# Attention stage: keys transposed in fp32 with the low part taken from the bank, and state products in fp32

## The chip, the cores and the metric

The kernel runs on one core of one Trainium2 chip. The metric is the device time of one execution in microseconds (us); less is better. The three runs shown of the kernel before took 1138.49, 1142.32 and 1143.38 us, median 1142.32.

## What is computed

The program computes a retention layer (attention without a softmax, with a decay for each head), and two mixture-of-experts layers behind it. The change touches the first layer alone:

```python
# q, k, v: [8 batches, 8 heads, 576 positions, 64], float32
scores = (1 / sqrt(64)) * q @ k.transpose(0, 1, 3, 2)
gamma  = 1.0 - 2.0 ** (-5.0 - arange(8))            # one decay for each head
Dmat   = where(i >= j, gamma ** (i - j), 0.0)       # i, j: positions
attn   = (scores * Dmat) @ v
x      = attn, as [4608 tokens, 512]
x      = moe(x)     # 8 experts, each token to its best one
out    = moe2(x)    # 8 experts, each with a fixed share of the tokens
```

## The kernel before

**Tiles.** The 4608 tokens are cut into 36 tiles of 128, all 8 heads of a tile at once. A batch has four whole tiles and a tail of 64 positions; the tails of two batches share a tile, so 32 tiles are whole and 4 are tails. Inside a tile the scores are computed outright (`scores`, `outputs`). What earlier tiles of the batch add comes from a 64x64 state for each head, the decayed sum of the products of keys and values, which `kv` carries from tile to tile (tails need no new state).

**Precision.** TensorE multiplies float16. Each fp32 operand is kept as a high part and a low part (the rounding error of the high part), and a product is the sum of three: high by high, high by low, low by high.

**Stages.** The list `stages` (L304) names what is done in a step of the loop at L305, and with which lead: loads 6 tiles ahead (`load`), decayed values on GpSimd 4 ahead (`pre`, `vf`), splits of k and v 3 ahead (`kvsplit`), transposes of q and k 2 ahead (`trans`), scores 1 ahead, then state (`kv`), `outputs` and the scaled rows `xr` (`rows`), the transposed rows 1 behind (`xtrans`) and the logits of the router 2 behind. A scheduler with a model of the engines sets the final order on each queue, so the order of the code isn't that of the engines.

**The key's way before.** ScalarE writes the high part `kh` of the loaded k (L146), VectorE the low part `kl` (L147), both with the positions on partitions. TensorE turns both in float16, eight transposes of 128x128 into one PSUM bank (L176), and ScalarE copies the bank to SBUF as `kT` in one instruction of 128x1024 (L177). `kv` multiplies `kh`, `kl` with `vh`, `vl`: 24 float16 products a tile, each with 64 columns of weights and 64 moving columns, two heads side by side on the two halves of the partitions (L230).

**The query's way**, for comparison: four fp32 transposes (`across`, L156), ScalarE takes the high part from the bank (L162), TensorE subtracts it in the bank (L163), ScalarE takes the rest (L164). The rows `xr` go the same way.

**PSUM.** `tp` has three banks that transposes of q, k and rows and the logits share; `pS` (two banks, one buffer) holds the scores, `pO` (two banks) the output, `pk` one bank the state's products. `pS` is used thus: 24 score products (L189), VectorE writes the masked high part `sh` (L192), TensorE subtracts it in the bank (L194), VectorE writes the low part `sl` (L196); only then do the next tile's scores start.

Of the kernel before, what the change touches and what calls it, by code (L numbers as in the profile page):

```python
# [9 lines left out]
F32 = mybir.dt.float32  # L10
F16 = mybir.dt.float16
I32 = mybir.dt.int32
AF = mybir.ActivationFunctionType
OP = mybir.AluOpType
# [27 lines left out]
def consts_np():  # L42
    import numpy as np
    p=np.arange(128)
    g=1.0-2.0**(-5.0-np.arange(8))
    cols=[]
    cols.append((g[None,:]**(127-p)[:,None])*256.0)
    cols.append((g[None,:]**(63-p%64)[:,None])*256.0)
    cols.append((g[None,:]**(p-127.0)[:,None])*2.0**-21)
    cols.append((g[None,:]**((p%64)-63.0)[:,None])*2.0**-21)  # L50
    hd=(np.arange(4)[None,:]*2+(p[:,None]//64))
    cols.append(g[hd]**128*2.0**-6); cols.append(g[hd]**64*2.0**-6)
    tok=np.zeros((128,36))
    for t in range(36):
        pr,k=divmod(t,9)
        if k<8:
            c,bi=divmod(k,2); tok[:,t]=(2*pr+bi)*576+c*128+p
        else: tok[:,t]=(2*pr+p//64)*576+512+p%64
    cols.append(tok)
    cols.append(np.eye(128))  # L60
    j=p[:,None]; i=p[None,:]
    cols.append((i>=j)*2.0**-6)
    cols.append(((i>=j)&((i//64)==(j//64)))*2.0**-6)
    cols.append((j<i)*1.0)
    cols.append((1.0*p)[:,None])
    cols.append((p[:,None]//16==np.arange(8)[None,:])*1.0)
    cols.append((p[:,None]%16==np.arange(16)[None,:])*1.0)
    return np.ascontiguousarray(np.concatenate(cols,1).astype(np.float32))
# [32 lines left out]
def attention(k, q, kk_, v, wg1, X, after):  # L101
    tc, nc = k.tc, k.nc
    from contextlib import ExitStack
    ctx = ExitStack()
    ld = ctx.enter_context(tc.tile_pool(name="ld", bufs=4))
    wk = ctx.enter_context(tc.tile_pool(name="wk", bufs=3))
    xp = ctx.enter_context(tc.tile_pool(name="xrp", bufs=4))
    ps = ctx.enter_context(tc.tile_pool(name="aps", bufs=1, space=bass.MemoryType.PSUM))
# [18 lines left out]

    def load(d):
        for src, name in ((kk_, "k"), (q, "q"), (v, "v")):
            t = ld.tile([128, 8, 64], F32, name=name, bufs=5 if name == "q" else 3)  # L130
            if d.tail:
                for bi in range(2):
                    nc.sync.dma_start(t[bi * 64:(bi + 1) * 64], src[2 * d.pr + bi, :, 512:576, :].rearrange("h p d -> p h d"))
            else:
                nc.sync.dma_start(t, src[d.b, :, d.c * 128:(d.c + 1) * 128, :].rearrange("h p d -> p h d"))
            setattr(d, "i" + name, t)

    def pre(d):

        d.vf = wk.tile([128, 8, 64], F32, name="vf", bufs=3)  # L140
        nc.gpsimd.tensor_tensor(d.vf, d.iv, k.c('gkt' if d.tail else 'gk')[:, :, None].to_broadcast([128, 8, 64]), op=OP.mult)

    def kvsplit(d):
        d.kh = wk.tile([128, 8, 64], F16, name="kh", bufs=5)
        d.kl = wk.tile([128, 8, 64], F16, name="kl", bufs=4)
        nc.scalar.activation(d.kh, d.ik, AF.Copy, scale=256.0)  # L146
        nc.vector.scalar_tensor_tensor(d.kl, d.ik, 256.0, d.kh, op0=OP.mult, op1=OP.subtract)  # L147
        d.vh = wk.tile([128, 8, 64], F16, name="vh", bufs=4)
        d.vl = wk.tile([128, 8, 64], F16, name="vl", bufs=4)
        nc.scalar.activation(d.vh, d.vf, AF.Copy)  # L150
        nc.gpsimd.tensor_tensor(d.vl, d.vf, d.vh, op=OP.subtract)  # L151

    def across(pt, x):

        for c in range(4):
            nc.tensor.matmul(pt[:, c, :], x[:, c * 128:(c + 1) * 128], idf, is_transpose=True, start=c == 0, stop=False,  # L156
                             skip_group_check=True)

    def split(h, l, pt):

        f = lambda x: x.rearrange("p c i -> p (c i)")
        nc.scalar.activation(h, pt, AF.Copy, scale=256.0)  # L162
        nc.tensor.matmul(f(pt), k.less8, f(h), start=False, stop=True, skip_group_check=True)  # L163
        nc.scalar.activation(l, pt, AF.Copy, scale=256.0)  # L164

    def trans(d):
        d.qh, d.ql = (wk.tile([128, 4, 128], F16, name=x, bufs=4) for x in ("qTh", "qTl"))
        pt = ps.tile([128, 4, 128], F32, name="tp", bufs=3)
        across(pt, d.iq.rearrange("p a d -> p (a d)"))
        split(d.qh, d.ql, pt)  # L170
        kT = wk.tile([128, 2, 4, 128], F16, name="kT", bufs=2)
        d.kTh, d.kTl = kT[:, 0], kT[:, 1]
        pt = ps.tile([128, 2, 4, 128], F16, name="tp", bufs=3)
        for n, x in enumerate((d.kh, d.kl)):
            for hp in range(4):
                nc.tensor.transpose(pt[:, n, hp, :], x[:, 2 * hp:2 * hp + 2, :].rearrange("p a d -> p (a d)"), k.idh)  # L176
        nc.scalar.activation(kT, pt, AF.Copy)  # L177

    def scores(d):

# [17 lines left out]
    state = {}  # L198
# [22 lines left out]
    def kv(d):  # L221
        d.state = dict(state)
        if d.tail:
            return
        pk = ps.tile([128, 4, 64], F32, name="pk")
        for hp in range(4):
            for n, (x, y) in enumerate(((d.kh, d.vh), (d.kh, d.vl), (d.kl, d.vh))):
                for z in range(2):
                    h = 2 * hp + z
                    nc.tensor.matmul(pk[64 * z:64 * z + 64, hp, :], x[:, h, :], y[:, h, :], start=n == 0, stop=n == 2)  # L230
        f = k.c('gst' if d.c == 3 else 'gs')[:, :, None].to_broadcast([128, 4, 64])
        n32 = wk.tile([128, 4, 64], F32, name=f"st{d.bi}", bufs=2)
        nh = wk.tile([128, 4, 64], F16, name=f"sth{d.bi}", bufs=2)
        nl = wk.tile([128, 4, 64], F16, name=f"stl{d.bi}", bufs=2)
        if d.c:
            s1 = wk.tile([128, 4, 64], F32, name="s1", bufs=3)
            nc.vector.scalar_tensor_tensor(s1, state[d.bi][0], 64.0, pk, op0=OP.mult, op1=OP.add)
            nc.gpsimd.tensor_tensor(n32, s1, f, op=OP.mult)
        else:
            nc.vector.tensor_tensor(n32, pk, f, op=OP.mult)  # L240
        nc.scalar.activation(nh, n32, AF.Copy)
        nc.gpsimd.tensor_tensor(nl, n32, nh, op=OP.subtract)
        state[d.bi] = (n32, nh, nl)
# [55 lines left out]
    def store(n):  # L299
        for _ in range(min(n, len(pend))):  # L300
            t, xr = pend.pop(0)
            nc.sync.dma_start(Xv[:, t, :], xr)

    stages = [(load, -6), (pre, -4), (trans, -2), (xtrans, 1), (kvsplit, -3), (scores, -1), (kv, 0), (outputs, 0), (rows, 0), (logits, 2)]  # L304
    for s in range(-7, NT + 5):  # L305
        store(2 if s < NT + 2 else 36)
        for f, off in stages:
# [1285 lines left out]
def program(tc, q, kk, v, wg1, w11, w12, wg2, w21, w22, consts, out, dbg=None):  # L1593
    nc = tc.nc
    ctx = ExitStack()
    k = K()
    k.pin = False
    setup(k, tc, nc, ctx, consts)
    moe_setup(k, ctx)
    X = tc.dram_tile([128 * NT, W], F32, name="Xs")  # L1600
    X1 = tc.dram_tile([128 * NS, W], F32, name="X1s")
    LG = tc.dram_tile([128 * NS, 8], F32, name="LGsd")
    g1 = split_gate(k, wg1, "wg1")
    k.wgl = split_gate(k, wg2, "wg2")
    select_setup(k)
    k.w = {0: K()}
    attention(k, q, kk, v, g1, X, early(k, X, w11[0]))
    open_ffn(k)
    rest = moe1(k, X, X1, w11, w12)
    k.pin = False  # L1610
    overflow(k, X, X1, LG, w11, w12)
    k.wn, k.xn, k.yn = 8, 9, 0
    k.pin = True
    moe2(k, X1, w21, w22, out, rest)
    k.pin = False
    anew(k, X1, w21, w22, out)
    if dbg:
        dbg(k, X, X1, LG)
    k.fctx.close()
    ctx.close()  # L1620
# [25 lines left out]
```

## Time and profile before

| | us |
|---|---|
| median of three runs | 1142.32 |
| the profiled execution, its own time | 1138.98 |
| its span, first to last instruction | 1137.1 |
| masked scores `sh`, start of the first and of the last of 36 | 12.5, 223.6 |
| PE busy | 1063.3 |
| DVE busy | 679.8 |
| ACT busy | 512.0 |
| POOL busy | 351.7 |

PE is TensorE's products, PEld its weight loads, DVE is VectorE, ACT ScalarE, POOL GpSimd, SP the queue that issues nearly all transfers. A matmul's end is modelled and products are pipelined, so PE reads as busy for longer than its array works. The mean granted clock of TensorE is 0.983. The first 230 us are the attention stage; the mixture-of-experts layers take the rest.

### The profile page before, as it was taken

To read this page: it belongs to the slowest core of one execution; us is meant where nothing else is said; L and a number is where in the kernel's file an instruction comes from. 1 tells how busy PE (TensorE), PEld (TensorE's weight loads), DVE (VectorE), ACT (ScalarE), POOL (GpSimd) and SP (SyncE) were. 2 spreads that over 40 slices of the span, in tenths; PEclk is the share of its full clock that TensorE was granted. 3 is DMA by queue.
4 is the path that set the end of the run, shared out by engine and by line. 5 is a ranking of instruction groups with operands and counts; after the bars stand their busy time and mean duration, and the time that the engine had idled before them with its cause. 6 is when DMAs were issued, how large, how long until landed. Compare 5 with 4: busy or idle time off the path is not lost. (4 is left out here: it accounts for less than half of the span.)

```text
span 1137.1 us, 26608 instructions
## 1 busy us (share of the span) xinstructions
PE 1063.3 (94%) x10679; PEld 680.3 (60%) x10679; DVE 679.8 (60%) x1662; ACT 512.0 (45%) x887; POOL 351.7 (31%) x589
## 2 busy tenths in 40 slices
PE   6899999888999999999989999898999999899996
PEld 4677777645556565656457644556475656567573
DVE  5788788766466655656544366748575666634140
ACT  6788787646354445545433123323232322224231
POOL 6767566322203020202031023234233051441101
PEclk9999999989999999999989999899999999999998
DMA  9979885439767676767967024357375473784211
GB/s 233 241 184 238 186 194 132 104 113 235 184 161 198 145 195 166 195 159 206 241 144 126 19 91 143 116 140 162 117 214 143 137 184 109 185 205 138 90 62 44
DMA packets 307523, 178.37 MB, mean 157 GB/s; under 512 B 241408, under 2 KB 274176, under 8 KB 307392
## 3 DMA queue, kind: packets, MB, share of 16 engines
q1 hardware_dynamic: 296928, 144.24, 52.0%
q0 software_dynamic: 10464, 32.34, 9.1%
q8 instruction: 87, 1.43, 0.5%
q14 instruction: 44, 0.36, 0.1%
HBM read 116.82 MB, written 31.28 MB: 130 GB/s over the span
## 5 line engine op out<-in xcount | busy, mean ns | idle before, releaser
L505 PE MATMUL ph<-xT,w1h 128*128 128x320 f16 (+4 forms) x2048 | 369.9, 297 | 14.4 <-DVE sc L318 7.1
L505 PEld LDWEIGHTS <-w1h 128*128 128x128 f16 x2048 | 198.6, 99 | 89.5 <-issue 26.0
L505 PE MATMUL ph<-xT,w1l 128*128 128x320 f16 (+4 forms) x1024 | 231.7, 297 | 0.0
L531 PE MATMUL py<-w2h,hh 128*128 128x512 f16 x536 | 203.2, 379 | 4.3 <-DVE x1r L587 2.2
L531 PE MATMUL py<-w2l,hh 128*128 128x512 f16 x536 | 203.2, 379 | 0.0
L531 PE MATMUL py<-w2h,hl 128*128 128x512 f16 x536 | 203.2, 379 | 0.0
L531 PEld LDWEIGHTS <-hh 128*128 128x128 f16 x1072 | 103.1, 98 | 121.6 <-issue 6.3
L510 ACT ACTIVATE hh<-ph 128x576 f16<-128x576 f32 (+4 forms) x136 | 83.3, 614 | 178.7 <-PE ph L505 174.1
L511 DVE SCALAR_TENSOR_TENSOR hl<-ph,hh 128x576 f16<-128x576 f32 (+4 forms) x136 | 97.8, 719 | 66.1 <-ACT hh L510 64.9
L505 PEld LDWEIGHTS <-w1l 128*128 128x128 f16 x1024 | 100.0, 99 | 33.0 <-issue 1.6
L393 DVE SCALAR_TENSOR_TENSOR w1l<-stage,w1h 128x1024 f16<-128x1024 f32 x62 | 75.9, 1228 | 60.5 <-ACT w1h L390 59.4
L531 PEld LDWEIGHTS <-hl 128*128 128x128 f16 x536 | 52.4, 98 | 60.3
L393 DVE SCALAR_TENSOR_TENSOR w2l<-stage,w2h 128x1024 f16<-128x1024 f32 x64 | 78.4, 1225 | 10.2 <-ACT w2h L390 8.9
L436 ACT ACTIVATE x1r<-py 128x512 bf16<-128x512 f32 x40 | 23.8, 596 | 109.0 <-PE py L531 65.5
L390 ACT ACTIVATE w2h<-stage 128x1024 f16<-128x1024 f32 x64 | 67.0, 1049 | 6.8 <-DMA stage<-in_moe_w_dram 6.7
L390 ACT ACTIVATE w1h<-stage 128x1024 f16<-128x1024 f32 x62 | 64.2, 1046 | 9.4 <-DMA stage<-in_moe_w_dram 9.4
L1452 POOL DMA_INDIRECT out_dram<-w2T,ti x20 | 21.8, 1089 | 128.3 <-ACT w2T L1451 107.6
L589 POOL COPY x1r<-sc 128x1 f32<-128x1 f32 x37 | 8.3, 227 | 163.2 <-DMA X1s<-x1r 102.2
L1452 POOL DMA_INDIRECT out_dram<-x1r,ti x20 | 21.4, 1072 | 120.6 <-ACT x1r L1451 101.8
L424 POOL DMA_INDIRECT xg<-X1s,ix x40 | 45.2, 1129 | 43.1 <-DVE zf L1378 23.4
L192 DVE TENSOR_TENSOR sh<-pS,ct 128x1024 f16<-128x1024 f32 x36 | 43.8, 1217 | 16.1 <-PE pS L189 16.1
L151 POOL TENSOR_TENSOR vl<-vf,vh 128x512 f16<-128x512 f32 x36 | 42.6, 1186 | 31.4 <-ACT vh L150 30.9
(376 smaller groups left out, 1900.7 us busy)
## 6 DMA issues: line engine op xcount, KB each, us to landing
stage<-in_moe_w_dram SPq DMA_DIRECT2D x128, 512.0 KB, 4.2
Xs<-xr SPq DMA_DIRECT2D x36, 257.0 KB, 4.5
X1s<-x1r SPq DMA_DIRECT2D x33, 257.0 KB, 3.7
k<-in_k_dram SPq DMA_DIRECT2D x32, 256.0 KB, 4.0
q<-in_q_dram SPq DMA_DIRECT2D x32, 256.0 KB, 4.2
v<-in_v_dram SPq DMA_DIRECT2D x32, 256.0 KB, 4.2
q<-in_q_dram SPq DMA_DIRECT2D x8, 128.0 KB, 3.8
k<-in_k_dram SPq DMA_DIRECT2D x8, 128.0 KB, 4.9
```

The costliest lines, as they stand in the source:

```text
L151: nc.gpsimd.tensor_tensor(d.vl, d.vf, d.vh, op=OP.subtract)
L192: nc.vector.tensor_tensor(f(d.sh), f(pS), both, op=OP.mult)
L390: d = nc.scalar.activation(at(h, i), t, AF.Copy, scale=128.0)
L393: d = nc.vector.scalar_tensor_tensor(at(l, i), t, 128.0, at(h, i), op0=OP.mult, op1=OP.subtract)
L424: nc.gpsimd.indirect_dma_start(out=xg[:M], out_offset=None, in_=src, in_offset=bass.IndirectOffsetOnAxis(ap=gidx[:M], axis=0))
L436: d = nc.scalar.activation(q.bitcast(mybir.dt.bfloat16), x, AF.Square, accum_out=sc[:, 0:1])
L505: pe(k, nc.tensor.matmul(ph[:, z, :b], x[:, c, F], xT[:, y + c, a:a + b], start=i == 0, stop=i == 11))
L510: nc.scalar.activation(oh, src, AF.Relu)
L511: nc.vector.scalar_tensor_tensor(ol, src, 0.0, oh, op0=OP.max, op1=OP.subtract)
L531: pe(k, nc.tensor.matmul(py, x[:, f, S], y[:, f, :], start=i == 0, stop=i == 23))
L589: nc.gpsimd.tensor_copy(xr[:, 513:514], sc[:, 5:6])
L1452: nc.gpsimd.indirect_dma_start(out=out2 if tail else out, out_offset=bass.IndirectOffsetOnAxis(ap=ti, axis=0), in_=y, in_offset=None)
```

## The change

- ScalarE and VectorE no longer split the loaded k: `kh` and `kl` go, `kvsplit` becomes `vsplit`, for v alone.
- Four fp32 transposes turn the loaded k into a `tp` bank (L170 of the new file); ScalarE writes the high part `kTh` from the bank, 128x512, and VectorE writes the low part `kTl` from the bank and `kTh`, 128x512 (L172).
- `kv` multiplies the loaded k and the decayed v in fp32: 8 products a tile in place of 24. The scales of the state follow (k is no longer multiplied by 256).
- k and `vf` are now read by `kv` and so are held longer: 7 buffers for k in place of 3, 5 for `vf` in place of 3.

```diff
-    cols.append(g[hd]**128*2.0**-6); cols.append(g[hd]**64*2.0**-6)
+    cols.append(g[hd]**128*4.0); cols.append(g[hd]**64*4.0)
...
-            t = ld.tile([128, 8, 64], F32, name=name, bufs=5 if name == "q" else 3)
+            t = ld.tile([128, 8, 64], F32, name=name, bufs=dict(k=7, q=5, v=3)[name])
...
-        d.vf = wk.tile([128, 8, 64], F32, name="vf", bufs=3)
+        d.vf = wk.tile([128, 8, 64], F32, name="vf", bufs=5)
...
-    def kvsplit(d):
-        d.kh = wk.tile([128, 8, 64], F16, name="kh", bufs=5)
-        d.kl = wk.tile([128, 8, 64], F16, name="kl", bufs=4)
-        nc.scalar.activation(d.kh, d.ik, AF.Copy, scale=256.0)
-        nc.vector.scalar_tensor_tensor(d.kl, d.ik, 256.0, d.kh, op0=OP.mult, op1=OP.subtract)
+    def vsplit(d):
...
-        pt = ps.tile([128, 2, 4, 128], F16, name="tp", bufs=3)
-        for n, x in enumerate((d.kh, d.kl)):
-            for hp in range(4):
-                nc.tensor.transpose(pt[:, n, hp, :], x[:, 2 * hp:2 * hp + 2, :].rearrange("p a d -> p (a d)"), k.idh)
-        nc.scalar.activation(kT, pt, AF.Copy)
+        pt = ps.tile([128, 4, 128], F32, name="tp", bufs=3)
+        across(pt, d.ik.rearrange("p a d -> p (a d)"))
+        nc.scalar.activation(d.kTh, pt, AF.Copy, scale=256.0)
+        nc.vector.scalar_tensor_tensor(d.kTl, pt, 256.0, d.kTh, op0=OP.mult, op1=OP.subtract)
...
-            for n, (x, y) in enumerate(((d.kh, d.vh), (d.kh, d.vl), (d.kl, d.vh))):
-                for z in range(2):
-                    h = 2 * hp + z
-                    nc.tensor.matmul(pk[64 * z:64 * z + 64, hp, :], x[:, h, :], y[:, h, :], start=n == 0, stop=n == 2)
+            for z in range(2):
+                h = 2 * hp + z
+                nc.tensor.matmul(pk[64 * z:64 * z + 64, hp, :], d.ik[:, h, :], d.vf[:, h, :], start=True, stop=True)
...
-            nc.vector.scalar_tensor_tensor(s1, state[d.bi][0], 64.0, pk, op0=OP.mult, op1=OP.add)
+            nc.vector.scalar_tensor_tensor(s1, state[d.bi][0], 0.25, pk, op0=OP.mult, op1=OP.add)
...
-    stages = [(load, -6), (pre, -4), (trans, -2), (xtrans, 1), (kvsplit, -3), (scores, -1), (kv, 0), (outputs, 0), (rows, 0), (logits, 2)]
+    stages = [(load, -6), (pre, -4), (trans, -2), (xtrans, 1), (vsplit, -3), (scores, -1), (kv, 0), (outputs, 0), (rows, 0), (logits, 2)]
```

The scheduler orders the changed program anew. On VectorE, in the first third of the attention stage, before (numbers tell buffers apart; `pS_624` to `sh_622` to `sl_623` is one tile):

```order
L147 SCALAR_TENSOR_TENSOR kl_477<-k_205,kh_476 128x512
L192 TENSOR_TENSOR sh_622<-pS_624,ct_58 128x1024
L251 TENSOR_TENSOR xr_435<-pO_686,ct_58 128x2x4x64
L196 TENSOR_TENSOR sl_623<-pS_624,ct_58 128x1024
L147 SCALAR_TENSOR_TENSOR kl_615<-k_242,kh_614 128x512
L192 TENSOR_TENSOR sh_797<-pS_799,ct_58 128x1024
L251 TENSOR_TENSOR xr_435<-pO_861,ct_58 128x2x4x64
L147 SCALAR_TENSOR_TENSOR kl_790<-k_310,kh_789 128x512
L196 TENSOR_TENSOR sl_798<-pS_799,ct_58 128x1024
```

and of the change, in the same part of the stage (`kT` is written from the bank `tp`):

```order
L191 TENSOR_TENSOR sl_1010<-pS_1011,ct_58 128x1024
L172 SCALAR_TENSOR_TENSOR kT_1159<-tp_1160,kT_1159 128x512
L187 TENSOR_TENSOR sh_1181<-pS_1183,ct_58 128x1024
L245 TENSOR_TENSOR xr_953<-pO_1229,ct_58 128x2x4x64
L172 SCALAR_TENSOR_TENSOR kT_1313<-tp_1314,kT_1313 128x512
L191 TENSOR_TENSOR sl_1182<-pS_1183,ct_58 128x1024
L231 SCALAR_TENSOR_TENSOR s1_1378<-st1_1049,pk_1366 128x256
L187 TENSOR_TENSOR sh_1335<-pS_1337,ct_58 128x1024
L245 TENSOR_TENSOR xr_953<-pO_1383,ct_58 128x2x4x64
```

The low part of the key stands at the same places, once a tile between `sl` and the next `sh` or between `xr` and `sl`; it now waits for a bank and for ScalarE's `kTh`.

On TensorE, around the transposes of q and k, before, in the second half of the stage:

```order
L156 MATMUL tp<-ct,q 128x128 x4
L176 LDWEIGHTS kh
L176 MATMUL tp<-idh,kh 128x128
...
L176 LDWEIGHTS kl
L176 MATMUL tp<-idh,kl 128x128
...
L230 LDWEIGHTS kh
L230 MATMUL pk<-vh,kh 64x64
...
L194 LDWEIGHTS less_65
L194 MATMUL pS<-sh,less_65 128x512
```

and of the change:

```order
L152 MATMUL tp<-ct,q 128x128 x4
L152 MATMUL tp<-ct,k 128x128 x4
L224 MATMUL pk<-vf,k 64x64 x8
L189 LDWEIGHTS less_65
L189 MATMUL pS<-sh,less_65 128x512
```

All eight fp32 products can now stand ahead of the subtraction in `pS`, where before two of the 24 small ones did and the others came after it. (In other tiles they stand behind it, in both programs.)

## Rows read from the trace of the kernel before

**Rows 1.** Busy time by stretch: us, then PE, PEld, DVE, ACT, POOL busy (instructions), clock, DMA share, GB/s.

```profile
20.00:220.00 200.00, 186.91 (x4072) 144.13 (x4073) 164.16 (x271) 159.89 (x316) 128.91 (x149) 1.00 0.78 190
20.00:60.00 40.00, 34.00 (x723) 25.85 (x724) 32.72 (x43) 31.16 (x58) 29.77 (x30) 1.00 0.97 242
...
300.00:1137.00 837.00, 796.84 (x5904) 487.36 (x5902) 457.60 (x1216) 304.84 (x481) 193.40 (x361) 0.98 0.57 147
```

**Rows 2.** The masked scores' line: count, shortest, median, longest ns; first and last start.

```profile
L192 DVE TENSOR_TENSOR sh<-pS,ct x36: 1193/1217/1225, 12.5 to 223.6; 128x1024 f16<-128x1024 f32 x36
```

**Rows 3.** Who waited for whom, 0 to 220 us: us in total, times, longest.

```profile
DVE sh L192 <- PE pS L189: 16.1, 16, 2.1
DVE kl L147 <- ACT kh L146: 13.3, 12, 4.2
```

**Rows 4.** Timeline of PE, 84.0 to 85.6 us: start, us from first start to last end.

```profile
84.11 0.66 PE L156 MATMUL tp<-ct,q 128*128 128x128 f32 x4
84.60 0.39 PE L176 MATMUL tp<-idh,kh 128*128 128x128 f16 x4
84.82 0.39 PE L176 MATMUL tp<-idh,kl 128*128 128x128 f16 x4
85.04 0.61 PE L156 MATMUL tp<-ct,xr 128*128 128x128 f32 x4
85.49 0.22 PE L219 MATMUL pO<-vh,sh 128*128 128x64 f16 x2
```

**Rows 5.** Timeline of PE, 82.4 to 83.0 us: the state's products of one tile.

```profile
82.44 0.22 PE L230 MATMUL pk<-vh,kh 128*64 128x64 f16 x2
82.50 0.20 PE L230 MATMUL pk<-vl,kh 128*64 128x64 f16 x2
...
82.81 0.20 PE L230 MATMUL pk<-vh,kl 128*64 128x64 f16 x1
```

**Rows 6.** The only fp32 product that isn't a transpose (one instruction): timeline, and its line.

```profile
624.31 0.29 PEld L1240 LDWEIGHTS tp<-bx,one_f 1*128 1x128 f32 x2 [0.26 <-issue]
L1240 PEld LDWEIGHTS tp<-bx,one_f x2: 181/182/184, 624.3 to 624.4; 1*128 1x128 f32 x2
L1240 PE MATMUL tp<-bx,one_f x2: 245/256/266, 624.3 to 624.4; 1*128 1x1 f32 x2
```

**Rows 7.** Groups of instructions, 0 to 330 us: busy us, mean ns | idle before.

```profile
L146 ACT ACTIVATE kh<-k 128x512 f16<-128x512 f32 x36 | 22.6, 627 | 3.8 <-DMA k<-in_k_dram 3.8
L177 ACT ACTIVATE kT<-tp 128x1024 f16<-128x1024 f16 x36 | 36.8, 1021 | 3.3 <-PE tp L176 2.6 <-PE pS L189 0.6
L162 ACT ACTIVATE qTh<-tp 128x512 f16<-128x512 f32 x36 | 21.4, 593 | 7.2 <-PE tp L156 7.0
L147 DVE SCALAR_TENSOR_TENSOR kl<-k,kh 128x512 f16<-128x512 f32 x36 | 34.4, 956 | 13.9 <-ACT kh L146 13.3 <-ACT lgs L270 0.4
L511 DVE SCALAR_TENSOR_TENSOR hl<-ph,hh 128x640 f16<-128x640 f32 x8 | 6.6, 823 | 2.3 <-ACT hh L510 2.3
L511 DVE SCALAR_TENSOR_TENSOR hl<-ph,hh 128x384 f16<-128x384 f32 x8 | 4.4, 551 | 1.5 <-ACT hh L510 1.5
```

**Rows 8.** The line of the key's low part: count, shortest, median, longest ns.

```profile
L147 DVE SCALAR_TENSOR_TENSOR kl<-k,kh x36: 674/744/2357, 6.5 to 190.9; 128x512 f16<-128x512 f32 x36
```

## Prediction

> **What bounds the kernel now.** I read the busy time by stretch first [rows 1]. The change touches only the attention stage, and its steady part is the stretch from 20 to 220 us. There PE is busy for 186.9 of 200 us, DVE for 164.2, ACT for 159.9 and POOL for 128.9, at a full granted clock. So PE comes first, with 13.1 us of idle time at the most, and two helpers follow at about 80%: none of them alone sets the pace. Then I read the masked scores' line [rows 2]: 36 of them start between 12.5 and 223.6 us, which makes 211.1 / 35 = 6.03 us a tile. What the change is worth is 36 times what it takes off or adds to that period. The transfers are no bound over the stage: their share is 0.78, and even from 20 to 60 us, where it is 0.97, PE doesn't wait for them but runs behind a full set of buffers. Behind 300 us the same products, weights and gathers follow as before, and the stretch [rows 1] moves as a whole with the end of attention; I cost it at nothing.
>
> The list of waits [rows 3] tells how the engines hang together: DVE waits 16.1 us for PE's scores and 13.3 us for ACT's high part of the key. A tile goes round a loop: scores on PE, `sh` on DVE, the subtraction on PE, `sl` on DVE, next scores. Whatever stands between these on PE or DVE lengthens the loop.
>
> **The change, part by part.**
>
> *Transposes of k on PE.* Eight float16 ones run from 84.60 to 85.04 us, 0.44 us a tile. Four fp32 ones take 84.60 - 84.11 = 0.49 us (with a late start) and 85.49 - 85.04 = 0.45 us [rows 4]. The difference is 0.01 to 0.05 us; I take 0. At 0.05 it would be 36 x 0.05 = 1.8 us.
>
> *State products on PE, 32 tiles.* The 24 float16 products start between 82.44 and 82.81 us, two heads within one start, so they take 0.40 us with the last one's own step of 0.03 [rows 5]. Eight fp32 ones replace them, and the trace has no such product with 64 columns. The lowest price comes from the fp32 transposes: 0.45 / 4 = 0.11 us for 128 columns, so 0.055 us for 64, and four pairs side by side take 0.22 us. But the one fp32 product that is no transpose [rows 6] is one instruction with two weight loads and two matmuls in the trace. Its second load starts 0.29 - 0.18 = 0.11 us after the first, for 128 columns of weights. With 64 columns I estimate 0.055 us a pass, two passes and 0.11 us a product. Pairs side by side then take 0.44 us, products one after the other 0.88 us, and if no load hides behind a matmul either, 1.76 us. I take 0.44, since the rows nearest to it, the float16 products of the same shape, do run in pairs: 32 x (0.44 - 0.40) = **+1.3 us**. The ends are 32 x (0.22 - 0.40) = -5.8 us and 32 x (1.76 - 0.40) = +43.5 us.
>
> The page "FP8 and Floating Point Precision" of the Trainium skill (TensorE Precision Notes) says that true fp32 takes four passes through the array, for the products of both halves of both operands. By it I estimate 4 x 64 columns at 2.4 GHz, 0.11 us a product, four times what the page would make of one float16 product; by the transposes' row it would be half. No row of this case shows the passes of a product with many moving columns.
>
> *DVE.* `kl` goes, 36 of 0.956 us mean [rows 7], and `kTl` of the same shape comes, read from the bank. The nearest rows are the low parts of the expert layers, also bank minus float16: 0.551 us for 384 columns and 0.823 for 640 [rows 7], so 0.687 for 512. That frees 36 x 0.269 = 9.7 us of DVE. Much of it is stretching: `kl` has a median of 0.744 and a longest of 2.357 us [rows 8], while `sh`, which reads a bank and one SBUF operand, keeps to 1.193 to 1.225 us beside the same GpSimd work [rows 2]. I count the freed time at DVE's busy share, 164.2 / 200 = 0.82, since where DVE stands idle anyway a shorter instruction gives nothing back: **-7.9 us**. The ends are 0 (PE sets the loop, DVE's gain becomes a longer wait for scores) and -9.7.
>
> Here the skill bears on a chance. "SBUF — State Buffer", section "Who interferes with whom", states that a VectorE instruction with two SBUF inputs contends with a GpSimd one that reads SBUF, and that one with at most one SBUF input doesn't. The two ranges in the rows agree. Without that rule `kTl` could be stretched like `kl`, and the sum would lose its 7.9 us.
>
> *ACT.* `kh` (0.627 us) and the copy `kT` (1.021) go, and a high part from the bank comes, like that of q (0.593) [rows 7]: 36 x 1.055 = 38.0 us of work less, from 80% busy to about 61%. I count none of it by itself. DVE's wait of 13.3 us for `kh` goes, but `kTl` waits for `kTh` from the same engine, and only after the transposes; where that wait returns in full, ACT's gain is idle time on ACT. The ends are 0 and -13.3 us.
>
> *Queues and buffers.* SP's order shifts: up to three more k loads stand ahead of the fourth and fifth v. At 242 GB/s [rows 1] 256 KB take 1.1 us, so v comes at most 3.3 us later, once, two tiles before its use: 0, at worst +3.3. POOL keeps all its instructions. k is now released by `kv` instead of the split, but has four buffers more; `vf` has two more for the same reason. The `tp` bank of k is read by two engines in turn, 0.593 + 0.687 us in place of 1.021, of three banks: 0.
>
> *Order on the loop.* The low part is made one tile ahead of its scores, so it doesn't sit between `sl` and the next scores by need. The fp32 products stand ahead of the subtraction in some tiles; there they delay `sl`, unless `sh` and `xr` on DVE cover them.
>
> **Sum.** +0 + 1.3 - 7.9 = -6.6 us against the profiled execution's own 1138.98, which is 3.3 us below the median of the runs shown: 1132.4, say **1132 us**. A measurement of this kernel tells about 0.5% from no change, 5.7 us: faster is below 1136.6, slower above 1148.0.
>
> **The rivals.**
>
> *No change.* Either the fp32 products don't pair: 32 x (0.88 - 0.40) = +15.4, with DVE's -7.9 makes 1146.5. Or they pair and PE takes up DVE's gain: +1.3 makes 1140.3. For it speaks that PE is at 93% busy; against it, that part of this is modelled, and that DVE and ACT are waited for in the loop.
>
> *Slower.* A weight load of fp32 can't hide behind the matmul of the pass before, and heads don't pair: 1.76 us a tile, +43.5 - 7.9 makes 1174.6. It decides from 32 x (x - 0.40) - 7.9 = 9.0, x = 0.93 us a tile. For it speaks that an fp32 load is long, 0.182 us for 128 columns [rows 6], and that the products can stand ahead of the subtraction, on the loop. Against it: the fp32 transposes follow each other at 0.11 us although each has its own load. Milder, 0.88 us and no gain on DVE makes 1138.98 + 15.4 = 1154.
>
> *More than the sum.* DVE's whole 9.7 us and its wait of 13.3 us for `kh` both come off the loop: 1138.98 - 23.0 = 1116. For it speaks that ACT falls by a quarter, so that high parts are ready earlier; against it, that PE had only 13.1 us of idle time to give, so that most of this would have to come from inside its busy time.
>
> **How the numbers follow.** The forecast with its better variant gets 0.48, all of it faster by over 0.5%. No change gets 0.27. Slower gets 0.25, about half of it at or below 1154 and half towards 1174. The range goes from 1116 to 1154: it leaves out that upper half, some 0.12, and 0.05 below. The likeliest case's own range is 1116 to 1136.
>
> **What would show each step.** If I am right, `sh` starts run from about 12 to 217 us, 5.85 us a tile. Four fp32 transposes of k take 0.45 us. The eight products show as 16 matmul rows within about 0.44 us, in pairs of equal start. `kTl` has a narrow spread near 0.69 us, and ACT is about 60% busy from 20 us on. The forecast is wrong if the products spread over 0.9 us or more a tile, if `sh` waits for scores much longer than 16.1 us in total, or if DVE's wait for ACT's high part comes back in full.

## The result, and the profile after

The changed kernel took 1123.05 us (median of five runs, 1122.38 to 1129.93); the kernel before took 1139.12 on the same chip (median of five). The ratio is 0.985, 95% interval 0.982 to 0.988. In four later comparisons on three other chips it was between 0.982 and 0.985. So the change is faster, as forecast, and the time lies inside the range, but the gain is 16 us where 7 were forecast. The profiled execution is the longest of its five, 1129.93 us, with a span of 1128.1.

Busy time by stretch, 20 to 220 us, of the kernel after (columns as in [rows 1]):

```profile
20.00:220.00 200.00, 188.45 (x3854) 149.00 (x3853) 158.78 (x283) 134.83 (x290) 118.04 (x148) 0.98 0.78 194
```

The 200 us hold 218 matmuls fewer than in [rows 1], though PE is further on in the program at their end; ACT falls from 159.9 to 134.8 us, POOL from 128.9 to 118.0. The clock, 0.98 in place of 1.00, is the mean over a stretch at half the full clock, 200.5 to 207.3 us, and the rest at the full one. The masked scores and the two new lines of the key (count, shortest, median, longest ns, first and last start):

```profile
L187 DVE TENSOR_TENSOR sh<-pS,ct x36: 1194/1225/1226, 13.4 to 213.0; 128x1024 f16<-128x1024 f32 x36
L172 DVE SCALAR_TENSOR_TENSOR kT<-tp,kT x36: 678/683/692, 9.5 to 205.8; 128x512 f16<-128x512 f32 x36
```

The scores' period is (213.0 - 13.4) / 35 = 5.70 us a tile, where 6.03 was read before [rows 2] and 5.85 forecast. The low part of the key is narrow, 0.683 us, where `kl` went up to 2.357 [rows 8]. Groups of instructions, 0 to 330 us (columns as in [rows 7]):

```profile
L172 DVE SCALAR_TENSOR_TENSOR kT<-tp,kT 128x512 f16<-128x512 f32 x36 | 24.7, 685 | 8.9 <-ACT kT L171 8.9
L224 PE MATMUL pk<-vf,k 128*64 128x64 f32 x512 | 24.0, 232 | 0.0
L171 ACT ACTIVATE kT<-tp 128x512 f16<-128x512 f32 x36 | 21.3, 593 | 5.7 <-PE tp L152 5.1 <-PE pS L184 0.6
```

Who waited for whom, 0 to 220 us:

```profile
DVE sh L187 <- PE pS L184: 17.2, 24, 2.7
ACT qTh L158 <- PE tp L152: 15.7, 23, 6.0
ACT xTh L158 <- PE tp L152: 15.4, 18, 2.8
...
DVE kT L172 <- ACT kT L171: 8.9, 8, 4.0
DVE sl L191 <- PE pS L189: 7.9, 14, 0.8
```

DVE's wait for a high part falls from 13.3 [rows 3] to 8.9 us; its wait for scores stays (17.2 here, 14.7 in a second profile, 16.1 before). ACT, which has 25 us less to do, waits longer for PE (15.7 and 15.4 us in two lines, where it was 7.0 and 7.8). So PE's own list is the place to look. Its timeline around one tile, after (start, us from first start to last end):

```profile
104.16 0.59 PE L189 MATMUL pS<-sh,less 128*128 128x512 f16 x2
104.60 0.49 PE L152 MATMUL tp<-ct,k 128*128 128x128 f32 x3
105.02 0.69 PE L224 MATMUL pk<-vf,k 128*64 128x64 f32 x16
105.63 0.66 PE L152 MATMUL tp<-ct,xr 128*128 128x128 f32 x4
```

and of the kernel before, with the state's products of one tile in two pieces:

```profile
100.49 0.39 PE L176 MATMUL tp<-idh,kl 128*128 128x128 f16 x4
100.81 0.22 PE L230 MATMUL pk<-vh,kh 128*64 128x64 f16 x2
...
100.92 0.20 PE L230 MATMUL pk<-vh,kh 128*64 128x64 f16 x2
101.05 0.61 PE L194 MATMUL pS<-sh,less 128*128 128x512 f16 x2
101.59 0.22 PE L230 MATMUL pk<-vl,kh 128*64 128x64 f16 x2
...
101.83 0.20 PE L230 MATMUL pk<-vh,kl 128*64 128x64 f16 x2
101.96 0.39 PE L163 MATMUL tp<-qTh,less 128*128 128x512 f16 x1
```

Look at the field behind the line's operands, 128*128, 128*64 or 64*128: the form in which the array is used. In the first fence two subtractions take 104.60 - 104.16 = 0.44 us, 0.22 each, and the next work of the same form follows at once. In the second the same two take 101.59 - 101.05 = 0.54 us, because products of another form come behind them: 0.1 us more. Four float16 transposes (0.22 us, [rows 4]) take 100.81 - 100.49 = 0.32 before the state's products. Leaving costs the same: two products that follow each other at 0.03 us are followed by the subtraction only 101.05 - 100.92 = 0.13 later. A step is the time from one product's start to the next one's. Taken over all rows, a step from an fp32 transpose to work of its own form has a median of 0.109 us, and to a state product of 0.203: **each change of form costs 0.094 us of PE**. Most other kinds of step grow by 0.093 to 0.1 us as well; those behind the router's products of eight columns grow by 0.07 (0.025 to 0.096), so the price is a little high for 18 of the changes before and 4 after.

### The profile page after: what moved, and what is told of

It reads as the page before. It is cut to its first block, busy times and chain, and to the rows that moved or that the text cites. A ratio compares the mean times of both kernels' runs of the same rounds, so it can differ in the third digit from the quotient of the medians.

```text
span 1128.1 us, 25795 instructions
## 1 busy us (share of the span) xinstructions
PE 1061.4 (94%) x10279; PEld 682.9 (61%) x10279; DVE 668.7 (59%) x1662; ACT 481.4 (43%) x851; POOL 340.7 (30%) x589
## 5 line engine op out<-in xcount | busy, mean ns | idle before, releaser
L499 PE MATMUL ph<-xT,w1h 128*128 128x320 f16 (+4 forms) x2048 | 374.3, 299 | 11.9 <-DVE sc L312 4.9
L525 PE MATMUL py<-w2h,hh 128*128 128x512 f16 x536 | 203.2, 379 | 2.8 <-DVE key L1268 2.2
L525 PE MATMUL py<-w2h,hl 128*128 128x512 f16 x536 | 203.2, 379 | 0.0
L418 POOL DMA_INDIRECT xg<-X1s,ix x40 | 44.7, 1116 | 44.2 <-DVE zf L1372 24.3
L187 DVE TENSOR_TENSOR sh<-pS,ct 128x1024 f16<-128x1024 f32 x36 | 43.9, 1220 | 17.3 <-PE pS L184 17.2
```

Of the source, the lines that this page charges most:

```text
L187: nc.vector.tensor_tensor(f(d.sh), f(pS), both, op=OP.mult)
L418: nc.gpsimd.indirect_dma_start(out=xg[:M], out_offset=None, in_=src, in_offset=bass.IndirectOffsetOnAxis(ap=gidx[:M], axis=0))
L499: pe(k, nc.tensor.matmul(ph[:, z, :b], x[:, c, F], xT[:, y + c, a:a + b], start=i == 0, stop=i == 11))
L525: pe(k, nc.tensor.matmul(py, x[:, f, S], y[:, f, :], start=i == 0, stop=i == 23))
```

## A ledger of PE's time

With that price PE's time from the first to the last masked score can be split into three: its own steps (each kind's shortest regular step times its count: 0.109 us an fp32 transpose, 0.056 a float16 one, 0.216 a product of 512 columns, 0.029 one of 64, and so on), the changes of form times 0.094, and the rest, which is waits and time lost to a lower clock for the most part. The last column has the time at half the full granted clock (1.2 in place of 2.4 GHz). In such a stretch fp32 transposes follow each other at 0.213 us in place of 0.109, so it costs half of its length at most.

| kernel | span | own steps | changes of form | times 0.094 | rest | us at half the clock |
|---|---|---|---|---|---|---|
| before, four profiles | 211.1 to 213.1 | 155.1 | 315 | 29.6 | 26.4 to 28.4 | 0 to 3.4 |
| after, five profiles | 198.7 to 201.3 | 156.8 | 211 | 19.8 | 22.1 to 24.7 | 0 to 6.8 |
| held | 206.3 | 155.0 | 233 | 21.9 | 29.4 | 0 |
| kv32 | 210.5 | 157.3 | 233 | 21.9 | 31.3 | 3.4 |
| turn32 | 216.3 | 154.9 | 312 | 29.3 | 32.1 | 6.8 |
| act_fill | 204.2 | 156.8 | 225 | 21.1 | 26.3 | 3.4 |
| dve_fill | 203.2 | 156.8 | 211 | 19.8 | 26.6 | 3.4 |
| kv_twice | 228.8 | 170.6 | 297 | 27.9 | 30.2 | 6.8 |
| q_like_k | 213.3 | 148.6 | 195 | 18.3 | 46.4 | 23.9 |
| few_blocks | 226.5 | 157.3 | 135 | 12.7 | 56.5 | 9.2 |
| many_blocks | 249.9 | 157.1 | 576 | 54.1 | 38.7 | 30.7 |

Between the means of before (212.2) and after (199.7) lie -12.5 us: own steps +1.7, changes of form -9.8, the rest -4.4 (27.5 to 23.1). The two profiles with the full clock throughout, 211.1 before and 198.7 after, give the same, -12.4. Of the 104 changes fewer, 77 are into and out of the state's products, which stood in 72 pieces among other work before and in 36 after (15 to 210 us); the other 27 are at the products of 64 rows, which the scheduler orders anew too. All operands of eight fp32 products are ready at once, while the 24 float16 ones need `kh`, `kl`, `vh` and `vl`; that this is why the scheduler keeps the eight together is read from the program, not tested. (The expectations below count the whole list of the stage, which has 7 to 12 changes more. Of the kernels made for a test there is one profile each, and the profiles of after alone differ by 2.6 us.)

## The experiments

Between them the kernels ran on five chips, on all but the first of which the median of before was 1151 to 1153 us, so ratios and attention spans are compared rather than times of different sets.

**After_again: the change as it is.**

> The changed kernel as it is, once more with a profile and times. Where did the gain of about 16 us come from? Theory 'all in attention': the first expert product starts 10 to 16 us earlier than before (before 232.4 us in its profiled execution, the first profile of the change 221.6 us), and the stretch from there to the end of the span is as long as before, 904.7 us, within 2 us. Theory 'part of it behind attention': the stretch behind is 3 to 6 us shorter than before's in an execution with a time near the median of 1123. Time: 1120 to 1126 us.

Measured: 1130.66 us, ratio 0.982 (0.978 to 0.986). The first expert product starts at 219.7 us, and 906.1 us lie behind it. So 12.7 us of the gain lie in attention against the first profile of before, and the stretch behind was not shorter than its 904.7. The time itself is above the 1120 to 1126 expected, as this chip's before is, 1151.74.

**Act_fill: ScalarE's old load put back.**

```diff
+        xa = wk.tile([128, 8, 64], F16, name="xa", bufs=2)
+        nc.scalar.activation(xa, d.ik, AF.Copy, scale=256.0)
+        nc.scalar.activation(xa[:, 0:4], d.ik[:, 0:4], AF.Copy, scale=256.0)
```

> The changed kernel with two spare ScalarE copies of the loaded k for each tile, 128x512 and 128x256, about 1.05 us together, so that ScalarE does as much as before the change; nothing reads them. Theory 'ScalarE's relief is worth the missing 5 to 10 us' (the forecast counted its 38 us at nothing): the gain of the change shrinks by 5 to 10 us, to a time of 1128 to 1133 us, and VectorE's and TensorE's waits for ScalarE grow. Rival 'VectorE alone, in full': within 2 us of the changed kernel, 1121 to 1125 us. Rival 'order': a change of either sign of up to 3 us without a wait for ScalarE behind it.

Measured: 1134.94 us, 4.3 above the changed kernel in the same set. The spare work is 36 x (0.626 + 0.416) = 37.5 us:

```profile
L145 ACT ACTIVATE xa<-k 128x512 f16<-128x512 f32 x36 | 22.5, 626 | 3.8 <-DMA k<-in_k_dram 3.8
L146 ACT ACTIVATE xa<-k 128x256 f16<-128x256 f32 x36 | 15.0, 416 | 0.4
```

Attention is 4.5 us longer than the mean of after, 1.3 of it from 14 more changes of form and 3.2 in the rest. ScalarE's relief is worth something, though less than the 5 to 10 us of that theory and more than the 2 us of its rival.

**Dve_fill: VectorE's load put back.**

```diff
+        xv = wk.tile([128, 8, 64], F16, name="xv", bufs=2)
+        nc.vector.scalar_tensor_tensor(xv[:, 0:2], d.ik[:, 0:2], 256.0, d.ik[:, 2:4], op0=OP.mult, op1=OP.subtract)
```

> The changed kernel with one spare VectorE instruction for each tile, 128x128 from two SBUF inputs, an estimated 0.27 us, which is what the low part of the key became shorter by; nothing reads it. Theory 'VectorE's 9.7 us count nearly in full': 8 to 10 us slower than the changed kernel, 1131 to 1133 us. Forecast's own term: 7.9 us slower, 1131 us. Theory 'ScalarE gave the gain and VectorE little': 0 to 4 us slower, 1123 to 1127 us.

```profile
L145 DVE SCALAR_TENSOR_TENSOR xv<-k 128x128 f16<-128x128 f32 x36 | 17.2, 479 | 1.1 <-DMA k<-in_k_dram 1.1
```

The spare instruction took 0.479 us, not the 0.27 estimated: it puts back 17.2 us, 1.8 times what the change frees. The time is 1140.04 us, 9.4 above the changed kernel of the same set, but attention is only 3.5 us longer than the mean of after, all of it in the rest; the remainder lies behind attention (913.2 us in place of 906.1 in after_again), where PE's instructions are in the order of the changed kernel, and its cause is open. So in attention this DVE work was waited for at about 3.5 / 17.2 = 0.20 of its length, not at the 0.82 of the forecast; in the whole time it is 0.55.

**Kv_twice: the state's products doubled.**

```diff
+                for _ in range(2):
+                    nc.tensor.matmul(pk[64 * z:64 * z + 64, hp, :], d.ik[:, h, :], d.vf[:, h, :], start=True, stop=True)
```

> The changed kernel with each fp32 product of the state issued twice (the second overwrites the first with the same result). If PE sets the pace wherever these products stand, 32 tiles times 0.44 to 0.50 us of one set is added: 14 to 16 us slower, 1137 to 1139 us. If they lie in PE's gaps between the scores and their low parts: 0 to 7 us slower, 1123 to 1130 us. If the second product of a place has to wait for the first one's drain, more than 16 us.

Measured: 1170.21 us, 39.5 above the changed kernel, the outcome "more than 16", but not for the reason given with it: the rows of the doubled products still run in pairs, 0.058 us a pair. The ledger has the cause. Own steps grow by 13.8 us; the scheduler cuts the longer run of products in 74 pieces in place of 36, 86 changes of form more, 8.1 us; the rest grows by 7.1. That makes 29.0 in attention, and the other 10 lie behind it. This run was the first hint that pieces matter:

```profile
109.54 0.56 PE L225 MATMUL pk<-vf,k 128*64 128x64 f32 x10
110.03 0.66 PE L152 MATMUL tp<-ct,xr 128*128 128x128 f32 x4
...
110.95 0.45 PE L225 MATMUL pk<-vf,k 128*64 128x64 f32 x6
```

**Held: the arithmetic of before, its state products held together.**

```diff
-            for n, (x, y) in enumerate(((d.kh, d.vh), (d.kh, d.vl), (d.kl, d.vh))):
...
+        with tc.high_priority(offset=1000):
...
+                for n, (x, y) in enumerate(((d.kh, d.vl), (d.kl, d.vh), (d.kh, d.vh))):
```

> The kernel before, with the arithmetic of before; only the order of TensorE's work is moved: the 24 float16 state products of a tile get a higher priority in the scheduler and begin with those that need the latest operand, so that they stand together. In PE's list of the attention stage the changes of the array's form (64 rows, 64 columns or the whole array) fall from 324 to 241. Theory 'each change of form costs 0.094 us on PE' (read from the traces of before and after: the step from a 128x128 transpose to a product of 64 columns is 0.203 us against 0.109 to one of its own form): 83 fewer, 7.8 us faster than before, a ratio near 0.993; the attention stage is 6 to 9 us shorter. Rival 'the gain of the change comes from VectorE's and ScalarE's relief': as before, within 2 us.

Measured: 1145.27 us, ratio 0.9964 (0.9944 to 0.9983). Attention is 5.9 us shorter than the mean of before (4.8 shorter than the profile of before that, like this one, has the full clock throughout): 7.7 from changes of form, of which the rest takes 1.9 back. The order alone thus gives a gain, in the whole time about half of the 7.8 us expected. The rival (within 2 us of before without VectorE's and ScalarE's relief) falls, but only just: the interval of the ratio ends at 0.9983, which is 2 us.

**Kv32: the fp32 products alone.** The state's products of the change in the kernel before; key, splits and float16 transposes as before. The buffers are those of the change, and `kh` and `kl` have 3 each in place of 5 and 4; what that costs was not tried alone.

```diff
+                nc.tensor.matmul(pk[64 * z:64 * z + 64, hp, :], d.ik[:, h, :], d.vf[:, h, :], start=True, stop=True)
...
-            nc.vector.scalar_tensor_tensor(s1, state[d.bi][0], 64.0, pk, op0=OP.mult, op1=OP.add)
+            nc.vector.scalar_tensor_tensor(s1, state[d.bi][0], 0.25, pk, op0=OP.mult, op1=OP.add)
```

> The kernel before with the fp32 state products alone (and the buffers, with fewer for the split key); the key is split and turned as before, so that VectorE and ScalarE have all their old work. Forms change 244 times in place of 324. Theory 'changes of form': -80 times 0.094 is -7.5 us, the eight fp32 products themselves take 0.52 in place of 0.40 us a tile, +3.9: 3.6 us faster than before. Forecast's own steps: 1.3 us slower. Rival 'all of the gain is VectorE's and ScalarE's': no faster, 0 to 4 us slower.

Measured: ratio 1.0017 (0.9996 to 1.0038): no gain. Changes of form give 7.7 us, as foreseen, but own steps take 2.2 and the rest 3.8, which leaves attention 1.6 us shorter than the mean of before. Who waited, 0 to 225 us:

```profile
DVE kl L147 <- ACT kh L146: 14.5, 14, 1.6
...
DVE sh L192 <- PE pS L189: 12.5, 16, 1.7
```

With `kh` and `kl` still made, the wait of DVE for ACT is all there (13.3 before [rows 3]), and DVE waits less for PE (16.1 before). That PE's freed time turned into waits for the helpers fits this; fewer buffers for `kh` and `kl` would fit it too.

**Turn32: the turning alone.** The changed kernel, with float16 state products, so that `kh` and `kl` are made as well.

```diff
+        nc.scalar.activation(d.kh, d.ik, AF.Copy, scale=256.0)
+        nc.vector.scalar_tensor_tensor(d.kl, d.ik, 256.0, d.kh, op0=OP.mult, op1=OP.subtract)
...
-                nc.tensor.matmul(pk[64 * z:64 * z + 64, hp, :], d.ik[:, h, :], d.vf[:, h, :], start=True, stop=True)
+                    nc.tensor.matmul(pk[64 * z:64 * z + 64, hp, :], x[:, h, :], y[:, h, :], start=n == 0, stop=n == 2)
```

> The other part alone: the key is turned in fp32 and its low part made from the bank, but the state's products stay in float16, so that the key's split with positions on partitions stays as well (kh and kl are made too). Forms change 319 times (324 before), VectorE does 24.6 us more, ScalarE 15.4 us less. Theory: the fewer blocks come from the fp32 state products alone, and VectorE's added work is waited for at 0.3 to 0.8 of its length: 6 to 18 us slower than before. Rival 'the turning is what gives the gain': faster than before by 5 us or more.

Measured: ratio 0.9982 (0.9959 to 1.0006): the same as before, below the 6 us of the theory and far from the gain of the rival. Attention is 4.2 us longer than the mean of before, with 24.6 us of VectorE's work more, ScalarE's less and changes of form as before (312); of the 4.2 us up to 2.1 are the lower clock. DVE waits for ScalarE's high parts no longer than before, 8.4 + 4.2 us in place of 13.3 (0 to 225 us):

```profile
DVE kT L176 <- ACT kT L175: 8.4, 8, 2.3
...
DVE kl L147 <- ACT kh L146: 4.2, 6, 1.1
```

**Neither part gains alone.** The fp32 products bring few pieces, and only with both parts can `kh` and `kl` go; that the helpers then keep up with a shorter PE list is the reading that fits, and no run has the order of the change together with the helpers' old work in full.

**Q_like_k: q treated as k.**

```diff
-        split(d.qh, d.ql, pt)
+        nc.scalar.activation(d.qh, pt, AF.Copy, scale=256.0)
+        nc.vector.scalar_tensor_tensor(d.ql, pt, 256.0, d.qh, op0=OP.mult, op1=OP.subtract)
```

> The changed kernel with q treated as k is: its low part is made by VectorE from the bank, and TensorE's subtraction and ScalarE's second read of q go. PE's own work falls by 36 times 0.216 = 7.8 us, forms change 207 times in place of 220 (1.2 us), ScalarE does 21 us less, VectorE 24.6 us more. At the price that the spare VectorE work showed in attention (5.3 us for 17.2 us) VectorE costs 7.6 us and ScalarE gives 3: about 4 us faster than the changed kernel. At the forecast's price, VectorE's busy share of 0.82, it costs 20 us: some 8 us slower.

Measured: 1153.16 us, ratio 0.9991 (0.9968 to 1.0014): the whole gain of the change is lost. PE's own steps fall by 8.2 us and changes of form by 1.5, yet the rest doubles, from 23.1 to 46.4. Both sums of the expectation, 4 us faster and 8 us slower than the changed kernel, missed. The new group (columns as in [rows 7]):

```profile
L167 DVE SCALAR_TENSOR_TENSOR qTl<-tp,qTh 128x512 f16<-128x512 f32 x36 | 24.8, 688 | 19.1 <-ACT qTh L166 19.1
```

DVE stands 19.1 us before this one line, with `sh`, `sl` and `xr` behind it in its queue. That is not all: the attention stage has 23.9 us at half the clock, where the profiles of the change have 3.4 on average. Busy time by stretch, in such a part and beside one (columns as in [rows 1]):

```profile
36.00:43.00 7.00, 6.33 (x91) 4.89 (x91) 4.14 (x6) 3.15 (x6) 6.79 (x7) 0.51 1.02 223
46.00:53.00 7.00, 7.00 (x168) 5.74 (x168) 6.63 (x15) 4.71 (x11) 4.03 (x6) 1.00 0.96 246
```

So of the 23.3 us that the rest gains, up to (23.9 - 3.4) / 2 = 10 are the clock, and 13 or more are waits. It is no chance of one execution: the mean clock of all ten is 0.967 to 0.977, and that of the changed kernel's 0.978 to 0.985. Why this kernel gets the lower clock more often is not shown. The same 24.6 us of VectorE's work that goes with 4 us in turn32, where DVE's waits for ScalarE didn't grow, goes with 23 in the rest here.

**Few_blocks and many_blocks: the arithmetic of after in other orders.** Both only set priorities, 1000 ahead, few_blocks around the state's and the output's products, many_blocks around the scores' and the output's.

```diff
+        with tc.high_priority(offset=1000):
+            for n, (z, o, x, y) in enumerate(both):
+                nc.tensor.matmul(o, x, y, start=n < 2, stop=n >= len(both) - 2, skip_group_check=True)
```

> The changed kernel with its arithmetic; the output products and the state products get a higher priority in the scheduler, so that forms change 142 times in place of 220. Theory 'changes of form': 78 times 0.094 is 7.3 us faster than the changed kernel, unless new waits take its place (outputs that stand ahead of the subtraction can delay the loop by a microsecond or two): 5 to 8 us faster, a ratio to before of about 0.975. Rival: as the changed kernel, or slower by the waits that the other order brings.

> The changed kernel with its arithmetic; scores and output products get the same high priority, and the scheduler interleaves them: forms change 583 times in place of 220. Theory 'changes of form, 0.094 us each': 363 more, 34 us slower than the changed kernel, all of it in the attention stage. Rival 'the array changes its form beside other work or in waits': slower by less than 10 us.

Many_blocks took 1185.37 us, ratio 1.031 (1.026 to 1.036); attention is 50.2 us longer than the mean of after, where 34 were expected: 365 changes more make 34.3, the rest grows by 15.6. Up to 13.6 of these are the clock, which is at half for 30.7 us of the stage. One product of each form in turn:

```profile
104.59 0.20 PE L216 MATMUL pO<-vh,sl 128*128 128x64 f16 x1
104.72 0.23 PE L185 MATMUL pS<-qTl,kT 64*128 64x128 f16 x1
104.88 0.20 PE L216 MATMUL pO<-vh,sl 128*128 128x64 f16 x1
105.02 0.23 PE L185 MATMUL pS<-qTl,kT 64*128 64x128 f16 x1
```

They stand 0.13 to 0.16 us apart, where a product behind one of its own form follows at 0.03 to 0.05. Few_blocks missed: 1169.68 us, ratio 1.016 (1.012 to 1.020), with the fewest changes of all. What its PE waited for (0 to 245 us):

```profile
PE pO L215 <- DVE sl L191: 10.9, 14, 1.4
PE tp L159 <- ACT xTh L158: 10.6, 23, 1.0
```

In after_again (0 to 215 us) the second wait was 2.6 us and the first isn't among the longest six. Output products that are moved ahead stand in PE's queue until `sl` is there, and everything behind them stands too. Fewer changes of form are worth 0.094 us each only if no wait takes their place. No kernel of the study is faster than the change.

**Behind attention: two profiles of each kernel on one chip, and one of each on another.**

> The kernel before, for a profile on the same chip as a profile of the change. On two other chips its median was 12 us higher than in the runs shown. Theory 'the attention stage is the same on every chip': from the first to the last masked score 210 to 212 us, the first expert product at 231 to 233 us; what is longer lies behind. If so, the stretch behind attention is 914 to 919 us in place of 904.7.

> The changed kernel, for a profile on the same chip. Theory: from the first to the last masked score 197 to 200 us, the first expert product at 219 to 222 us, so 10 to 13 us of the gain lie in attention on every chip. If the remainder of the gain (5 to 8 us) is a property of the change, the stretch behind is 5 to 8 us shorter than that of before on this chip; if it is the chance of single stalls, it differs from it by less than 3 us or in the other direction.

> The kernel before once more, beside the change on one chip, for the part of the gain that lies behind attention. Theory 'chance of single stalls': the stretch behind attention is 905 to 917 us and overlaps with that of the change. Theory 'property': it is 4 to 8 us longer than the change's in both pairs of profiles.

> The changed kernel beside it. Attention, from the first to the last masked score: 197 to 200 us. Behind attention: 905 to 908 us as in the three profiles so far if it is a property of the change, and up to 915 us if it is chance.

> A second profile of the kernel before in the same call, with the same two expectations.

> A second profile of the changed kernel in the same call, with the same two expectations.

Attention is nearly the same on every chip: 212.7, 213.1 and 211.8 us for before, 199.0, 200.0 and 201.3 for after (210 to 212 and 197 to 200 were expected; 212.7 and 201.3 lie outside). From the first expert product to the end, before takes 904.7, 910.6, 917.8 and 919.1 us (the first is the profile shown), after 906.6, 906.1, 907.1, 909.9 and 911.4. The means differ by 4.8 us, and the pairs of these later calls by 3.5, 7.9 and 7.7, but the two profiles shown above differ by 1.9 the other way, and the values overlap: 910.6 is below the 914 expected of before_again, and the forecast of "905 to 908 as in the three profiles so far" failed for after_b and after_c. PE's instructions are in the same order there in every kernel of the study, and the test kernels spread as widely, from 906.9 (act_fill) to 919.0 (few_blocks). The clock doesn't settle it: before has 37.7 to 47.7 us at half of it behind attention, after 35.7 to 44.4, about 1 us apart in the mean. That this part belongs to the change is therefore likely but not shown, and what would shorten it stays open.

## Why the prediction was right or wrong

**The direction was right, the size was not.** The sum was -6.6 us; attention gave -12.5, and the whole time -16.

*Transposes of k, "I take 0".* Right: own steps of turning fall from 15.6 to 14.8 us in the ledger, -0.8.

*State products, "I take 0.44, pairs side by side".* The mechanism was right: 16 rows in pairs, 0.058 us a pair, no wait for a weight load, so the rival Slower fell, and with it the half of No change in which the products don't pair. Their own steps cost 14.4 - 11.9 = +2.5 us, where +1.3 were put; a product takes 2 x 0.058 = 0.116 us beside its neighbour, where 0.11 was estimated. **But this is the step that failed.** The sum had no term for changes of form. I priced the 24 float16 products by one tile where they stand together [rows 5], as 0.40 us, and took that for all 32. In all but 3 tiles they stood in two or more pieces, and each piece costs 2 x 0.094 us for the changes of form, which is not in those rows. The term for the changes of form, put at nothing, measured -9.8 us: 77 x 0.094 = 7.2 at the state's products, 2.5 at others. It is larger than any that stood in the sum. The row that would have shown it is the step between the last subtraction and a state product, 0.54 us for two where two take 0.44. The page "TensorEngine Tiling (Array Packing)" of the Trainium skill (Key Properties) says that a change of tiling mode drains TensorE. It gives no price; the rows here, which show no drain as such, agree with it in the 0.094 us that each change costs. With that term the sum would have been -6.6 - 9.8 = -16.4. That this is close to the gain in the whole time is luck: attention gave 4 us less, and the other 4 us lie behind it.

*DVE, "at DVE's busy share, -7.9".* The duration was right (0.685 us mean, forecast 0.687). The price wasn't a busy share: the same engine's work was waited for at about 0.20 of its length in dve_fill's attention stage, and in q_like_k at half of its length or more (13 of 24.6 us, without the clock). The rest of the ledger, where both helpers' relief has to show, fell by 4.4 us in all, where 7.9 were put.

*ACT, "I count none of it by itself".* Too low, though by less than the first theory had it: act_fill costs 3.2 us in the rest and 4.5 in attention. DVE's wait for the high part came back in good part, 8.9 of 13.3 us. By the two fillings ACT's relief would be worth about 3 us and DVE's 0.20 x 9.7 = 2, together near the 4.4; that is an estimate from single profiles, and no run parts the two in the change itself. Without the changes of form the terms measured 1.7 - 4.4 = -2.7 us, less than a time can tell from no change: that the change came out clearly faster is owed to the term that the sum lacked.

*Queues and buffers, 0.* The period fell, and DVE's and PE's longest waits name no new transfer, so no cost shows there; the buffers weren't tried alone.

*Behind attention, "I cost it at nothing".* Open: the means differ by 4.8 us, as said above, and the profiles overlap.

*The rival More than the sum* (1116) was argued against with PE's 13.1 us of idle time, "most of this would have to come from inside its busy time". That is just where it came from: a change of form reads as busy time, since the ends of the matmuls are modelled. Attention from PE's side was never 93% work: own steps are 155.1 of 212.2 us, 73%. Attention's gain, 12.5 us, stayed below those 13.1 all the same.

*What would show each step.* Narrow `kTl`, the pairs (0.52 us for the eight products with the last step, 0.44 forecast) and the wait for scores at 17.2 us (16.1 before) came as written. ACT is at 67% where about 60 was forecast; the period, 5.70 for 5.85, was the one that told that a term was missing.

## What to carry to other kernels

When products of unlike forms share TensorE, count how many times the form changes in its list, not only the products: a change that needs fewer operands lets a scheduler keep a group together, and that can be worth more than the work it removes. Price a group by all its places, not by the one where it stands undisturbed, and split PE's "busy" into steps, changes and waits before you take idle time for the most that can be won. And an engine's added work has no one price: the same 24.6 us on VectorE went with 4 us where its waits for ScalarE didn't grow, and with 13 or more where it stood 19.1 us before that one line with the loop's work queued behind it. Look at the granted clock before you call a difference a wait.

## What was not expected of the hardware

- A change of the array's form costs 0.093 to 0.1 us of PE, alike for 64 rows and for 64 columns, in and out (0.07 behind products of eight columns), and is hidden in what reads as busy: 315 of them were 29.6 us of a stage of 212.
- The granted clock differs between kernels that compute the same: at half for 0 to 6.8 us of the change's attention stage, for 23.9 in q_like_k and for 30.7 in many_blocks.
- An fp32 product of 64x64 with 64 moving columns shows as two weight loads and two matmuls of 0.029 us a row in pairs; eight of them take about 0.5 us.
- GpSimd got faster with no edit of its own: the mean of `vf` fell from 1.183 to 1.054 us and that of `st` from 0.711 to 0.616, as VectorE's `kl`, with two SBUF inputs, went. Whether that is the cause is not shown: in turn32, which keeps `kl`, `vf` takes 1.092 and `st` 0.946. POOL's lines after (columns as in [rows 7]):

```profile
L141 POOL TENSOR_TENSOR vf<-v,ct 128x512 f32<-128x512 f32 x36 | 37.9, 1054 | 4.2 <-DMA v<-in_v_dram 4.0 <-POOL xr L290 0.2
L232 POOL TENSOR_TENSOR st<-s,ct 128x256 f32<-128x256 f32 x24 | 14.8, 616 | 11.7 <-DVE s L231 10.2 <-PE pS L189 1.4
```
